# Two-engine first casts, unbroken fillers, W1 by row blocks and a new order of loads in an attention-plus-MLP kernel

## The chip, the cores and the metric

The kernel runs on one core of a Trainium2 chip. The core has a matrix engine (TensorE, PE in the profile; its weight loads are shown as PEld), three elementwise engines (VectorE: DVE, ScalarE: ACT, GpSimd: POOL), and queues that issue transfers, of which SyncE's (SP) carries nearly all here. The engines run side by side, each takes its own instructions in the order in which they were written, and semaphores hold one back until what it reads is there.

The metric is the device time of one execution in microseconds (us): the median of several runs. Times inside an execution come from one profiled execution and are counted from its first instruction.

## The reference

Eight batches, eight heads, 576 positions, head size 64. Sliding-window causal attention (each position sees itself and the 63 before it) is followed by a layer norm, a two-layer MLP with ReLU, and a residual:

```python
mask = (rel >= 0) & (rel < window)            # window = 64
scores = np.where(mask, scale * q @ k.T, -1e9)
x = softmax(scores) @ v                       # heads side by side: (8, 576, 512)
xn = (x - mean) / sqrt(var + 1e-6) * g_ln
out = x + relu(xn @ w_ch1) @ w_ch2            # 512 -> 2048 -> 512
```

Everything goes in and out in fp32; inside, the matmuls take fp16.

## The kernel before, in words

**Tiling.** Of each batch the first 512 positions are one group (g = 0 to 7) of four row blocks of 128 (kb or j = 0 to 3); the last 64 positions of all batches ("tails") make up a ninth group. For a group: `load_qk` and `load_v` fetch q, k, v in fp32, `cast_qk` and `cast_v` turn them into fp16 on POOL, `t_main` transposes q and k on PE and an elementwise engine copies the result out of PSUM (`evac`: 0 is ACT, 1 is DVE). `s_pe` makes the scores of one row block, `s_exp` the exponentials on ACT, `s_mask` the masking on DVE (in batch 0 a matmul with a bias masks instead: `pe_mask`). `b_pe` multiplies by the values; a ones column in the value tiles gives the softmax sum. `b_rows` on DVE does the division, the mean and the variance; `z_step` subtracts the mean, `zt_step` transposes the result on PE into zT. `s_mm` is `s_pe` with `s_exp`, `b_step` is `b_pe` with `b_rows`.

**Two value tiles.** A block's windows need the values in two alignments: vA holds the positions as they are, vB holds them shifted by 64. For batches 0 and 1 vB is filled by copies of half a tile (`vB_cur`, `vB_prev`) out of the fp32 staging v32; later batches do it with transfers.

**The MLP.** `mlp_units(g)` gives a list of units that PE does one after the other. For group 0: eight units `l1_half` (two hidden blocks of 128 for half of the positions, eight matmuls of 128x256), eight units `l1` (one hidden block for all 512 positions, four matmuls of 128x512), ten units `l2_three` (the second layer of row blocks 0 to 2, staggered, two to six matmuls of 128x512) and four of `l2` for row block 3. A ReLU on ACT empties each PSUM bank; there are two banks for it (`mm`).

**Order.** The schedule is written out by hand. Ahead of the main loop (lines 797 to 896) stand the loads, the casts and the whole attention of batch 0, but for the last value step. In the loop over groups, `at(i, f, ...)` puts a piece of the next batch's attention behind unit i. So with group 0's units go the transposes, scores and value steps of batch 1, with group 1's those of batch 2, and so on. `keep_clock(n)` puts n matmuls of 128x512 that nobody reads between pieces of batch 0's attention, where PE would sit still.

**W1 and W2.** W1 is loaded in eight pieces of 512 KB (`w1_load`), multiplied by the layer norm's gain gT and cast on POOL (`w1_cast`); gT is made on PE from the gain row (`gps`). Pieces 2q and 2q+1 are the upper and lower half of the rows of one quarter of the columns, so a hidden block of that quarter needs both. W2 follows in eight pieces (`w2_load`, `w2_cast`); the first four share four staging buffers with W1's first four, and the last one reuses the buffer of W2's first.

**SP's queue.** All these loads stand in one queue in program order, stores of the output too. In the kernel before, batch 1's first q, k and first half of v go ahead of W2, its second half behind it, batch 2's q and k after that, and batch 2's v behind group 0's first stores.

The functions that the change touches, and the main program, with the line numbers of the profile:

Of the kernel before, what the change touches and what calls it, by code (L numbers as in the profile page):

```python
# [20 lines left out]
def kernel(  # L21
# [10 lines left out]
    nc = tc.nc  # L32
# [88 lines left out]

    def cast_qk(b, half, xs=(0, 1)):
# [13 lines left out]

    def load_v(b, c0, c1):
        if c0 == 0:
            v32[b] = p_in.tile([128, 4, H, D], FP32, tag="v32", name=f"v32_{b}", bufs=1)
        for c in range(c0, c1):  # L140
            nc.sync.dma_start(
                out=v32[b][:, c],
                in_=v[b, :, 128 * c:128 * c + 128, :].rearrange("h s d -> s h d"),
            )

    def cast_v(b, c0, c1):
        nc.gpsimd.tensor_copy(out=vA[b][:, c0:c1, :, 0:D], in_=v32[b][:, c0:c1])
# [10 lines left out]
    def vB_cur(b, c, eng):  # L158
        evac(eng, vB[b][64:128, c, :, 0:D], v32[b][0:64, c])

    def vB_prev(b, c, eng):
        evac(eng, vB[b][0:64, c + 1, :, 0:D], v32[b][64:128, c])
# [12 lines left out]
    def w1_load(i):  # L175
        q2, pr = divmod(i, 2)
        if i < 4:
# [11 lines left out]
    def w1_cast(i):  # L189
        q2, pr = divmod(i, 2)  # L190
        t = wst.pop(("w1", i))
        dst = w1g[:, 2 * pr:2 * pr + 2, (HID // 4) * q2:(HID // 4) * (q2 + 1)]
# [158 lines left out]
    def b_rows(g, kb):  # L351
# [22 lines left out]
        if g < 2 and (g, kb) != (0, 2):  # L374
            z_step(g, kb)
# [74 lines left out]
    def mlp_units(g, split=0, three=False, seven=True):  # L450
# [157 lines left out]

        def l2_three(i):
# [129 lines left out]
        for half in range(2):  # L739
            for i in range(split // 2):  # L740
                units.append(lambda half=half, i=i: l1_half(half, i))
# [62 lines left out]
    for i in range(8):  # L804
        w1_load(i)
    make_identity(nc, ident16)
    nc.vector.memset(mask, 1.0)
# [14 lines left out]
    def keep_clock(n):  # L822
        m = mbias[:, :]
        mb = bass.AP(tensor=m.tensor, offset=m.offset, ap=[m.ap[0], [0, 8], m.ap[1]])
        for _ in range(n):
            nc.tensor.matmul(out=warm[:, :].rearrange("p (a i) -> p a i", i=64), lhsT=ident16, rhs=mb,  # L826
                             start=True, stop=True)

    keep_clock(4)
    gps = ps_mm.tile([128, DM], FP32, tag="mm", name="gps")  # L830
# [3 lines left out]
    nc.vector.tensor_copy(out=gT, in_=gps[:, 0:NKC])  # L834
    for b in range(2):
        alloc_qkT(b)
        alloc_v(b)
        init_vB(b)
    cast_qk(0, 0)
    cast_v(0, 0, 1)  # L840
    cast_v(0, 1, 2)
    cast_qk(0, 1)
    cast_v(0, 2, 3)
    cast_v(0, 3, 4)
    nc.gpsimd.tensor_copy(out=vB[0][64:128, 3, :, 0:D], in_=v32[0][0:64, 3])
    for i in range(8):
        w1_cast(i)

    keep_clock(1)
    t_main(0, 0, 0)  # L850
    keep_clock(2)
    t_main(0, 1, 0)
    keep_clock(4)
    s_mm(0, 0, True)
    vB_cur(0, 0, 1)
    vB_prev(0, 0, 1)
    vB_cur(0, 1, 1)
    vB_prev(0, 1, 1)
    keep_clock(3)
    s_mm(0, 1, True)  # L860
    b_step(0, 0)
    keep_clock(2)
    vB_cur(0, 2, 0)
    t_main(0, 0, 1, 0)
    keep_clock(1)
    t_main(0, 1, 1, 0)
    keep_clock(2)
    b_step(0, 1)
    keep_clock(2)
    vB_prev(0, 2, 0)  # L870
    s_mm(0, 2, True)
    zt_step(0, 0)
    b_step(0, 2)
    zt_step(0, 1)
    s_mm(0, 3, True)
    z_step(0, 2)


    load_qk(1, 0)
    load_v(1, 0, 2)  # L880
# [3 lines left out]
    cast_v(1, 0, 1)  # L884
    cast_v(1, 1, 2)
    for i in range(8):
        w2_cast(i)
        if i == 0:
            w2_load(7)
    load_qk(1, 1)  # L890
# [5 lines left out]
    load_qk(2, 1)  # L896

# [7 lines left out]
    for g in range(NGRP):  # L905
# [19 lines left out]
        if g == 0:  # L925
            at(0, b_step, 0, 3)
            at(1, zt_step, 0, 2)
            at(3, zt_step, 0, 3, "dve")
# [3 lines left out]
            at(13, vB_cur, 1, 0, 1)  # L932
            at(13, vB_prev, 1, 0, 1)
            at(13, vB_cur, 1, 1, 1)
            at(13, vB_prev, 1, 1, 1)
# [6 lines left out]
            at(19, b_pe, 1, 0)  # L942
            at(19, b_pe, 1, 1, "sc")
            at(19, b_rows, 1, 0)
            at(20, b_rows, 1, 1)
            at(21, zt_step, 1, 0)
            at(23, zt_step, 1, 1)
# [206 lines left out]
```

## Time and profile before

| | |
|---|---|
| median of 3 runs | 303.9 us (303.8 to 305.1) |
| the profiled execution's own time | 305.16 us |
| its span, first to last instruction | 303.4 us |
| PE busy | 292.2 us, 96% of the span |
| DVE, POOL, ACT busy | 217.9, 166.5, 153.2 us |
| PE idle ahead of its first matmul | 2.32 us |
| first W1 unit starts | 20.93 us |
| first `l1` unit starts | 29.78 us |
| first `l2_three` unit starts | 37.58 us |
| first unit of group 1 starts | 56.03 us |
| matmuls of `keep_clock` | 21 |

Busy is the time in which an engine has an instruction under way. In the lists by time, each row gives the start, the length (of a run of like instructions together, if several are merged), the engine, the line, what is written and read, and in brackets the idle time just before it and what ended that. A matmul's end is modelled, so in a run of matmuls the distance from one start to the next is the better measure. A cast that waited for "DMA" began when its transfer landed.

### The profile page before, as it was taken

The page shows a single profiled execution, that of the slowest core. Times are in us where ns is not written, and L with a number is a line of the kernel's source. Part 1 is how long each engine was busy: PE and PEld are TensorE (multiplying, and loading weights), DVE is VectorE, ACT ScalarE, POOL GpSimd, SP SyncE. Part 2 cuts the span into 40 slices and gives each one's busy share as a digit, 9 for nine tenths or more (in the row PEclk, how much of TensorE's full clock was granted, in tenths as well). Part 3 has the DMA queues.
Part 4 walks back from the last instruction along what each step waited for, and adds up shares of the span by engine and source line. Part 5 has one row for each costly group of instructions (what it writes and reads, how often), then busy time and mean ns, then how long its engine had stood idle before and what let it go on. Part 6 is the DMA issues. An engine that isn't in the chain of part 4 may idle for free.

```text
span 303.4 us, 7577 instructions
## 1 busy us (share of the span) xinstructions
PE 292.2 (96%) x3061; PEld 196.4 (65%) x3061; DVE 217.9 (72%) x418; ACT 153.2 (50%) x257; POOL 166.5 (55%) x251
## 2 busy tenths in 40 slices
PE   6999989899999999999999999999999999999992
PEld 4457445598455478646964686469646854788881
DVE  0588596765855897669766875698568775789972
ACT  1496635578447742875167528842574056306400
POOL 7579676462550898198809962888048407115200
PEclk9999999999999999999999999999999999999999
DMA  8999999989967998799189997992729396003014
GB/s 190 263 382 309 325 366 273 304 238 250 154 167 232 245 204 176 260 266 176 36 259 294 199 177 240 291 160 56 219 52 174 71 204 161 19 23 135 0 38 104
DMA packets 113893, 58.35 MB, mean 192 GB/s; under 512 B 83649, under 2 KB 104705, under 8 KB 113858
## 3 DMA queue, kind: packets, MB, share of 16 engines
q1 hardware_dynamic: 113056, 55.60, 75.6%
q0 software_dynamic: 512, 1.86, 2.5%
q8 instruction: 24, 0.39, 0.6%
q10 hardware_dynamic: 290, 0.40, 0.5%
q14 instruction: 11, 0.09, 0.1%
HBM read 38.80 MB, written 9.44 MB: 159 GB/s over the span
## 4 chain that ended last, share of the span: by engine, by line
PE 90%; DVE 5%; ACT 2%; issue 0%; POOL 0%; POOLq 0%
PE hps L459 30%; PE pA L536 12%; PE pB L536 8%; PE pC L536 8%; PE hph L601 7%; PE ch L471 5%; PE xps L348 4%; PE sc L304 3%; PE tp L234 3%; PE lA L656 2%; PE ch L618 2%; DVE vB L222 2%; PE warm L826 2%; DVE pt L321 1%; ACT pt L314 1%; PE lC L656 1%
## 5 line engine op out<-in xcount | busy, mean ns | idle before, releaser
L459 PE MATMUL hps<-zT,w1g 128*128 128x512 f16 x416 | 94.7, 379 | 0.0
L463 ACT ACTIVATE hrT<-hps 128x512 f16<-128x512 f32 x104 | 62.4, 600 | 41.2 <-PE hps L459 37.8
L459 PEld LDWEIGHTS <-w1g 128*128 128x128 f16 x416 | 39.2, 98 | 45.4 <-issue 2.2
L314 ACT ACTIVATE pt<-sc 128x512 f16<-128x512 f32 x72 | 39.3, 600 | 23.2 <-PE sc L304 22.5
L392 POOL TENSOR_SCALAR rsz<-mvg 128x1 f32<-128x1 f32 x28 | 10.8, 384 | 66.3 <-DVE mvg L373 58.8
L536 PEld LDWEIGHTS <-sS 128*128 128x128 f16 x448 | 43.3, 98 | 5.0
L128 POOL CAST qk<-qk 128x1024 f16<-128x1024 f32 x32 | 35.8, 1130 | 9.5 <-DMA qk<-in_q_dram 5.1
L321 DVE TENSOR_TENSOR pt<-pt,mask 128x1024 f16<-128x1024 f16 x32 | 26.0, 817 | 17.9 <-ACT pt L314 17.9
L536 PEld LDWEIGHTS <-hrT 128*128 128x128 f16 x336 | 32.1, 98 | 6.4 <-ACT hrT L463 1.0
L220 ACT COPY qkT<-tp 128x1024 f16<-128x1024 f16 x16 | 16.1, 1013 | 27.2 <-PE tp L234 23.7
L536 PE MATMUL pC<-w2s,sS 128*128 128x256 f16 x224 | 26.9, 273 | 0.0
L536 PE MATMUL pA<-wT,sS 128*128 128x256 f16 x224 | 26.9, 273 | 0.0
L368 DVE TENSOR_TENSOR xn<-xps,rcp 128x512 f32<-128x512 f32 (+1 forms) x48 | 25.7, 556 | 0.8
L370 DVE BATCH_NORM_STATS2 stats<-xn 128x6 f32<-128x512 f32 x36 | 25.0, 695 | 1.2
L510 DVE TENSOR_TENSOR sS<-hrT 128x512 f16<-128x512 f16 (+1 forms) x40 | 24.4, 609 | 2.1 <-ACT hrT L463 2.1
L601 PE MATMUL hph<-zT,w1g 128*128 128x256 f16 x192 | 23.2, 273 | 0.7 <-DVE zT L422 0.5
L393 POOL TENSOR_TENSOR rsz<-rsz,mhalf 128x1 f32<-128x1 f32 x28 | 19.7, 704 | 2.3
L601 PEld LDWEIGHTS <-w1g 128*128 128x128 f16 x192 | 18.1, 98 | 3.4 <-DVE zT L422 0.7
L398 POOL TENSOR_SCALAR z<-xn,rsz 128x512 f16<-128x512 f32 x24 | 18.5, 771 | 2.5
L471 PE MATMUL ch<-w2s,hrT 128*128 128x512 f16 x80 | 18.8, 380 | 0.0
L348 PEld LDWEIGHTS <-pt 128*64 128x64 f16 x576 | 11.4, 110 | 11.0 <-issue 5.3
L364 DVE RECIPROCAL rcp<-xps 128x8 f32<-128x8 f32 (+1 forms) x48 | 7.8, 183 | 15.0 <-PE xps L348 14.9
(117 smaller groups left out, 445.4 us busy)
## 6 DMA issues: line engine op xcount, KB each, us to landing
out_dram<-xn SPq DMA_DIRECT2D x33, 256.0 KB, 2.5
qk<-in_q_dram SPq DMA_DIRECT2D x16, 512.0 KB, 5.5
qk<-in_k_dram SPq DMA_DIRECT2D x16, 512.0 KB, 6.8
v<-in_v_dram SPq DMA_DIRECT2D x32, 256.0 KB, 6.3
w2s<-in_moe_w_ch_dram SPq DMA_DIRECT2D x9, 512.0 KB, 9.4
w1s<-in_moe_w_ch_dram SPq DMA_DIRECT2D x4, 512.0 KB, 6.7
tk<-in_k_dram SPq DMA_DIRECT2D x8, 256.0 KB, 4.9
tv<-in_v_dram SPq DMA_DIRECT2D x8, 256.0 KB, 4.8
```

The costliest lines, as they stand in the source:

```text
L128: nc.gpsimd.tensor_copy(out=dst[:, :].rearrange("p (a j) e d -> p a e j d", j=j), in_=t[:, :].rearrange("p (a e j d) -> p a e j d", e=2, j ...
L314: nc.scalar.activation(out=o, in_=i, func=AF.Exp, bias=0.0, scale=scale)
L321: nc.vector.tensor_tensor(out=ptv, in0=ptv, in1=mb, op=ALU.mult)
L348: nc.tensor.matmul(out=tiles[h // n][64 * r:64 * r + 64, h % n, :D + 1], lhsT=pt[:, par, hp, r, :], rhs=rhs, start=True, stop=True)
L368: nc.vector.tensor_tensor(out=xn[:, n * i:n * i + n], in0=xps[:, :, 0:D], in1=rcp_b, op=ALU.mult)
L370: nc.vector.bn_stats(out=stats, in_=xv)
L459: nc.tensor.matmul(out=hps, lhsT=w1g[:, kc, 128 * hc:128 * (hc + 1)], rhs=zT[g][:, kc, :], start=(kc == 0), stop=(kc == NKC - 1),)
L463: nc.scalar.activation(out=hrT[:, hc, :], in_=hps, func=AF.Relu, bias=0.0, scale=1.0)
L471: nc.tensor.matmul(out=ch[kb], lhsT=hrT[:, hc, 128 * kb:128 * (kb + 1)], rhs=w2s[:, hc, :], start=(hc == 0), stop=(hc == NHC - 1),)
L510: nc.vector.tensor_tensor(out=o, in0=x, in1=y, op=op)
L536: nc.tensor.matmul(out=o, lhsT=a[:, c, 128 * p:128 * p + 128], rhs=wv[:, c, :], start=(first and (p == 0 or split_c) and c == 0), stop=(c ...
L601: nc.tensor.matmul(out=hps[:, e], lhsT=w1g[:, kc, 128 * hc:128 * (hc + 1)], rhs=zT[g][:, kc, 256 * half:256 * half + 256], start=(kc == 0) ...
```

## The change

There are six edits.

1. **First casts.** `cast_two` casts batch 0's first q and k in two halves, one on ACT and one on DVE, in place of POOL; `t_two` transposes each half into a tile of its own, and ACT and DVE copy one half each.
2. **Fillers.** `keep_clock` uses a tile of zeros (`wfill`) that DVE sets right at the start, both as weights and as data, in place of the identity and the mask's bias. Thirteen of them stand ahead of the first transpose; the others are moved. There are 28 in all.
3. **Batch 0's attention is reordered.** The first value step is ahead of the second score step, the gain's matmuls are behind it, the gain is copied by ACT, zT of blocks 0 to 3 is copied by DVE, the last value step is ahead of the units. POOL fills more of vB (four half-tile copies instead of one).
4. **W1 by row blocks.** Pieces 2 and 3 of W1 hold all 512 rows of an eighth of the columns each (256 columns), so that each serves two hidden blocks alone; POOL casts such a piece in four instructions of 128x256. Two of group 0's units become `l1_rows`: four hidden blocks for one row block of 128 positions (16 matmuls of 128x128).
5. **W2 ahead of batch 1's v, value steps in pairs.** In SP's and POOL's order W2's eight pieces come ahead of batch 1's v. The copies into vB for batch 1 go from DVE to ACT, behind unit 20; both first value steps go behind unit 22 (before: 19), and the scores of its last two blocks behind unit 29 (before: 28). Batch 1's last two value steps stand together behind unit 1 of group 1 (before: behind units 0 and 2). The subtractions of the mean for blocks 0 and 1 are placed on their own, the second one behind two residual additions on DVE.
6. **Batch 2's v.** It is loaded into the staging tiles of the tails (`tk32`, `tv32`), which are free then, right behind batch 2's q and k and ahead of group 0's stores; before it was behind the first three stores.

The diff, cut to its core:

```diff
+    def cast_two(b, x, half):
+        t = qk32.pop((b, x, half))
+        dst = p_in.tile([128, 8, 2, D], FP16, tag=f"qk16_{x}", name=f"qk16_{x}_{b}_{half}")
...
+        for a in range(2):
+            evac(a, o[:, 2 * a:2 * a + 2], i[:, 2 * a:2 * a + 2])
+    def t_two(b, x, half):
...
+        for a in range(2):
+            tp = t_tile([128, 4, 128], f"tp_{b}_{x}_{half}_{a}")
+            for i in range(4):
+                nc.tensor.transpose(out=tp[:, i, :], in_=src[:, 4 * a + i], identity=ident16)
+            evac(a, qkT[b][x][:, 2 * a:2 * a + 2, c0:c0 + 256].rearrange("c h (p j) -> c h p j", j=2),
+                 tp[:, :].rearrange("c (h j) p -> c h p j", j=2))
...
     def load_v(b, c0, c1):
-        if c0 == 0:
-            v32[b] = p_in.tile([128, 4, H, D], FP32, tag="v32", name=f"v32_{b}", bufs=1)
+        if c0 == 0 and b == 2:
+            v32[b] = [p_in.tile([128, 2, H, D], FP32, tag=tag, name=f"v32_{b}_{tag}", bufs=1) for tag in ("tk32", "tv32")]
+        elif c0 == 0:
+            v32[b] = [p_in.tile([128, 4, H, D], FP32, tag="v32", name=f"v32_{b}", bufs=1)]
...
     def w1_load(i):
+        if i in (2, 3):
+            t = p_wst.tile([128, NKC, HID // 8], FP32, tag="wld", name=f"w1s_{i}")[:, :, :]
+            wst[("w1", i)] = t
+            nc.sync.dma_start(
+                out=t, in_=moe_w_ch1[:, (HID // 8) * i:(HID // 8) * (i + 1)].rearrange("(c p) n -> p c n", p=128),
+            )
+            return
     def w1_cast(i):
+        if i in (2, 3):
+            for kc in range(NKC):
+                nc.gpsimd.tensor_scalar(out=w1g[:, kc, (HID // 8) * i:(HID // 8) * (i + 1)], in0=t[:, kc],
+                                        scalar1=gT[:, kc:kc + 1], scalar2=1.0, op0=ALU.mult, op1=ALU.mult)
+            return
...
-        if g < 2 and (g, kb) != (0, 2):
+        if g < 2 and (g, kb) not in ((0, 2), (1, 0), (1, 1)):
             z_step(g, kb)
+        def l1_rows(kb):
+            for i in range(2):
+                if kb == 2:
+                    rows_ps[i] = ps_mm.tile([128, 2, 256], FP32, tag="mm", name=f"hph_{g}_1_{i}")
+                c0 = 128 * (kb - 2)
+                for e in range(2):
+                    hc = 2 * i + e
+                    for kc in range(NKC):
+                        nc.tensor.matmul(
+                            out=rows_ps[i][:, e, c0:c0 + 128], lhsT=w1g[:, kc, 128 * hc:128 * (hc + 1)],
+                            rhs=zT[g][:, kc, 128 * kb:128 * kb + 128], start=(kc == 0), stop=(kc == NKC - 1),
+                        )
+                if kb == 3:
+                    nc.scalar.activation(out=hrT[:, 2 * i:2 * i + 2, 256:512], in_=rows_ps[i],
+                                         func=AF.Relu, bias=0.0, scale=1.0)
...
+        halves = [(half, i) for half in range(2) for i in range(split // 2)]
+        if g == 0:
+            halves = [(0, 0), (0, 1), (0, 2), 2, 3, (0, 3), (1, 2), (1, 3)]
...
     load_qk(1, 0)
-    load_v(1, 0, 2)
     for i in range(7):
         w2_load(i)
     cast_qk(1, 0)
-    cast_v(1, 0, 1)
-    cast_v(1, 1, 2)
     for i in range(8):
         w2_cast(i)
         if i == 0:
             w2_load(7)
+    load_v(1, 0, 2)
+    cast_v(1, 0, 1)
+    cast_v(1, 1, 2)
...
     load_qk(2, 1)
+    load_v(2, 0, 4)
...
         if g == 0:
-            at(0, b_step, 0, 3)
-            at(1, zt_step, 0, 2)
-            at(3, zt_step, 0, 3, "dve")
+            at(1, zt_step, 0, 2, "dve")
+            at(2, zt_step, 0, 3, "dve")
...
-            at(13, vB_cur, 1, 0, 1)
-            at(13, vB_prev, 1, 0, 1)
-            at(13, vB_cur, 1, 1, 1)
-            at(13, vB_prev, 1, 1, 1)
...
-            at(19, b_pe, 1, 0)
-            at(19, b_pe, 1, 1, "sc")
-            at(19, b_rows, 1, 0)
-            at(20, b_rows, 1, 1)
-            at(21, zt_step, 1, 0)
-            at(23, zt_step, 1, 1)
+            for c in range(2):
+                at(20, vB_cur, 1, c, 0)
+                at(20, vB_prev, 1, c, 0)
+            at(22, b_pe, 1, 0)
+            at(22, b_pe, 1, 1, "sc")
+            at(22, b_rows, 1, 0)
+            at(22, z_step, 1, 0)
+            at(23, b_rows, 1, 1)
+            at(24, zt_step, 1, 0)
+            at(25, z_step, 1, 1)
+            at(26, zt_step, 1, 1)
...
-            at(28, s_pe, 1, 2)
-            at(28, s_pe, 1, 3, False, "t")
+            at(29, s_pe, 1, 2)
+            at(29, s_pe, 1, 3, False, "t")
...
-            at(27, load_v, 2, 0, 4)
         if g == 1:
-            at(0, b_step, 1, 2)
-            at(2, b_step, 1, 3)
+            at(1, b_pe, 1, 2)
+            at(1, b_pe, 1, 3, "sc")
+            at(1, b_rows, 1, 2)
+            at(2, b_rows, 1, 3)
```

Batch 0's stretch after the change, in the order in which it is written (its calls alone): `keep_clock(13)`, `cast_two` and `t_two` of q, `keep_clock(4)`, `cast_two` and `t_two` of k, `keep_clock(1)`, POOL's casts, `s_mm(0, 0)`, three copies into vB, `keep_clock(3)`, `b_step(0, 0)`, `s_mm(0, 1)`, the gain, W1's casts, `t_main` of q's second half, `keep_clock(1)`, `b_step(0, 1)`, `t_main` of k's second half, `zt_step(0, 0)`, `keep_clock(2)`, `s_mm(0, 2)`, `zt_step(0, 1)`, `keep_clock(1)`, `b_step(0, 2)`, `s_mm(0, 3)`, `z_step(0, 2)`, `keep_clock(3)`, `b_step(0, 3)`.

## The prediction

> **What bounds the kernel now.** I read the busy rows first, then PE's instructions in order of time up to 60 us with the idle time before each, then the chain of waits, then POOL's casts (they tell when transfers land) and DVE's order.
>
> ```profile
> PE 292.2 (96%) x3061; PEld 196.4 (65%) x3061; DVE 217.9 (72%) x418; ACT 153.2 (50%) x257; POOL 166.5 (55%) x251
> DMA  8999999989967998799189997992729396003014
> ```
>
> PE is the bound, and transfers are busy without a break for the first eleven slices (83 us). PE's own order:
>
> ```profile
> 2.32 1.86 PE L826 MATMUL warm<-mbias,ident 128*128 128x512 f16 x4 [2.32 <-DVE mbias L819]
> ...
> 14.30 0.61 PE L826 MATMUL warm<-mbias,ident 128*128 128x512 f16 x2
> ...
> 20.93 1.05 PE L601 MATMUL hph<-zT,w1g 128*128 128x256 f16 x8
> ...
> 26.27 3.67 PE L601 MATMUL hph<-zT,w1g 128*128 128x256 f16 x32 [0.52 <-DVE zT L422]
> ...
> 43.54 0.22 PE L348 MATMUL xps<-vB,pt 128*64 128x65 f16 x1 [0.86 <-DVE pt L321]
> ...
> 57.66 0.22 PE L348 MATMUL xps<-vB,pt 128*64 128x65 f16 x1 [0.59 <-DVE pt L321]
> ...
> 58.32 1.91 PE L601 MATMUL hph<-zT,w1g 128*128 128x256 f16 x16 [0.21 <-DVE xn L481]
> ```
>
> Up to 20.9 us PE mostly fills time; from 26.3 it lacks 0.86, 0.59 and 0.21 us, and after 58.3 the list shows no idle time above 0.06 us. So only the time at which PE gets past about 60 us can change, and the end moves by as much. The landings, in POOL's list:
>
> ```profile
> 9.29 0.62 POOL L147 CAST vA<-v 128x512 f16<-128x512 f32 x1 [0.55 <-DMA v<-in_v_dram]
> ...
> 20.85 2.72 POOL L195 TENSOR_SCALAR w1g<-w1s,gT 128x512 f16<-128x512 f32 x4 [1.36 <-DMA w1s<-in_moe_w_ch_dram]
> ...
> 45.43 1.04 POOL L209 CAST w2s<-w2s 128x1024 f16<-128x1024 f32 x1 [1.04 <-DMA w2s<-in_moe_w_ch_dram]
> 47.18 1.04 POOL L128 CAST qk<-qk 128x1024 f16<-128x1024 f32 x1 [0.71 <-DMA qk<-in_q_dram]
> ```
>
> POOL waits for nearly every piece up to 57 us: the queue of transfers, not POOL, sets when W2 and batch 1 are there.
>
> **Part 1, first casts and fillers (edits 1, 2).** Fillers before run at 0.45 us each (four from 2.32 to 4.12), at 14.30 at 0.22. Now they need only DVE's memset and start at 1.1 us, not 2.32. Thirteen end at 1.1 + 13 x 0.45 = 6.95 if all are slow, at 3.96 if all are fast. q lands at 5.0 (POOL's first cast starts at 5.08); half a cast is 128x512, 0.62 (64x512 on ACT or DVE) to 0.72 (ACT's z of 128x512), so q's transposes start between 5.8 and 6.95; before 6.31. k lands at 6.9; cast, two transposes of four (0.22 to 0.43 each) and half copies (0.57 ACT, 0.42 DVE) give the first scores at 8.7 to 9.7 instead of 11.57: 1.9 to 2.9 us.
>
> [...]
>
> **Part 2, batch 0 to the units (edit 3).** A block costs DVE 2.44 us (14.41 to 16.85: reciprocal to z). The first value step comes after its own exponentials (two in 1.08), at 10.3 to 11.3 against 13.92. Then: gain matmuls (1.79 at the slow pace), q's second half (lands at 11.1, POOL casts to 12.2), value step 1 at 13.7 to 14.9, z of block 1 after 16.6 to 17.8, k's second half copied by ACT at 15.6, scores 2 at 15.7, value step 2 at 17.2 to 18.1, scores 3 and their exponentials, value step 3 at 19.65 to 20.55. So the first unit can start at 20.05 to 20.95. POOL's other chain: v's last piece lands at 15.2; three more half copies (0.61 each) end at 17.2 where the one before ended at 16.56; W1's first two pieces (2.71) are cast at 19.95. This hides behind PE's chain. The first unit is hardly earlier (20.93), but the value step (0.4 and a 0.26 wait) and the 0.52 stall are out of the units.
>
> **Part 3, W1 (edit 4).** Unit 0,2 needs piece 2 alone: landed 20.8, four casts of 128x256 (half of 0.69 each; at worst the whole, +1.4 us on POOL, which meets `l1` with no slack), ready at 22.3 when PE wants it at 22.0. Two units of 16 matmuls of 128x128 at 0.056 (eight transposes in 0.45) are 1.79 against 1.75 for those they replace. Eight units of 0.87, two zT transposes (0.45) and 0.3 of waits: `l1` starts at 27.8 to 28.7 against 29.78. **Gain so far 1.1 to 2.0; I take 1.7.**
>
> Piece rows shrink from 2 to 1 KB. From 50 to 58 us, with batch 2's 1 KB rows, the transfers moved 348 GB/s, from 35 to 43, W2's 2 KB rows, 389: a piece takes 1.51 instead of 1.35 us, so two pieces put 0.3 us on everything behind. [...]
>
> **Part 4, W2 and batch 1 (edit 5).** From 27.8: eight `l1` (0.863 each) and two transposes end at 35.6; units 16 to 22 are 36 matmuls of 0.216, 7.8, scores 0.57: **PE reaches batch 1's value steps at 43.95** (up to 44.9). W2 lands about two v pieces earlier (1.17 each, 8.12 to 9.29), so each of its casts ends 0.5 us or more before its unit. But v now is what comes last. All up to W2's piece 7 landed at 45.4 before, v included, so v's first piece lands at 45.4 - 1.17 + 0.3 = 44.5 at the latest end. At the early end 43.4: the transfers moved only 225 GB/s from 27 to 32 us, when SP spent 24.35 to 29.43 on issuing v's small pieces; if that gap (0.8 to 1.1 us) closes, all come sooner. The late end is made of the same loads' rows, so I take 44.1. ACT's half cast (0.62) and 0.1 of signalling: **value step 0 at 44.8, 0.85 us after PE is there.** The second one waits for the second piece and ACT's third copy: 46.0.
>
> Behind it the chain lies on DVE: from 45.25, block 0 (1.95, as 43.41 to 45.38), a residual addition (0.70), block 1 (1.88), two additions (1.40), the small subtraction (0.10): 51.3; z on ACT (0.72 and 0.1): zT of block 1 can be transposed at 52.1. PE's own work would bring it there at 46.4 + 1.30 + 0.86 + 0.22 + 0.43 + 0.45 + 0.86 = 50.5: **a wait of 1.6 us that was not there before** (z was ready at 48.3, PE came at 49.34). Queued behind it on PE are units 27 to 29, on ACT the copy of q's second half. Then 0.22 + 0.86 + 0.45 + 1.73 = 55.35, scores; four exponentials end at 57.8, the last mask (0.82 to 1.46) at 58.7 to 59.3, the last value step (0.45) at 59.15 to 59.75. Before, the same work (both value steps, two units of group 1) was done at 60.54 - 0.87 = 59.67. **Sum: -0.5 to +0.1, I take -0.3.** DVE's vB copies (4.11 us at 36.45, the wait of 0.86) are gone, but what they delayed now waits for v.
>
> **Part 5, batch 2's v (edit 6).** Nothing: its cast stands behind rstdg at 63.24 on POOL, later than any landing. The stores move back by up to 6.7 us (four v issues, 53.55 to 60.22); batch 2's rows that need their buffers start at 74.85.
>
> The sum is made against the profiled execution: 305.16, span 303.4, the 1.8 around it unchanged, so 304.9. That execution was 1.26 above the median of the runs; against 303.9 the change gives **303.6**. A measurement here tells about 0.5% (1.5 us) from no change.
>
> **Rivals.**
> *The early gain is kept.* If v lands before 43.3, the first wait goes: value step 0 at 43.95, all 0.85 earlier, 302.7. If the DVE chain does not bind either, another 1.6: 301.1, and near 300.3 if the 1.66 of old waits is lost whole. For: the gap at 27 to 32 us. Against: 6.9 us of DVE and ACT work stand against 4.1 of PE between the same two points. Chance of 302.4 or less 0.2.
> *v lands late (slower).* v's issue is now behind that of W2's last piece, which waits for W2's first cast; then come 256 B rows, and batch 1's q is served beside them. If v comes with q, at 47.1 (POOL's row at 47.18), value step 0 starts at 47.8, 3 us later: 306.6. It decides from 45.9 on (1.5 us more than forecast plus the 0.3). For: W2's last piece took 9.9 us from issue (35.52) to cast. Against: the queue works in order wherever POOL's rows show it. Chance 0.17.
> *The clock stays slow.* Zeros might not count as work. Then PE's steps from 9 to 20 us double (about 3 us on its chain) and the units run slow until real work has opened the clock, some 7 us (as from 5.9 to 13 before; half lost: 3.5); less the 0.85 of slack: +5.6, 309.2. The trace has no matmul on zeros. Chance 0.07.
> *Forecast*, 0.56: 302.5 to 304.9 (v from 43.4 to 44.5, late start of the units, the mask's two prices).
>
> **Numbers.** Faster by 0.5%: the first rival, 0.20. Slower: the next two, 0.24. Same: 0.56. The range leaves out the ends of both sides: 302.0 to 306.3.
>
> **What would show it.** Fillers at 1.1 us and the pace of 0.22 before 8 us; first unit near 20.5; `l1` near 28; POOL's W2 casts about 2 us earlier and v's behind them at 44; an idle row ahead of the first value step of batch 1 (vB by ACT), one of 1 to 2 us ahead of block 1's zT transposes (z by ACT); group 1's third unit near 59.5. It is wrong if that unit starts off by more than 1.5 us, or if idle time appears after 60 us.

## The result and the profile after

| | before | after |
|---|---|---|
| median | 303.93 us (10 runs, 303.46 to 305.1) | 305.55 us (10 runs, 305.33 to 306.51) |
| ratio | | 1.0057, 95% interval 1.0044 to 1.007 |
| the profiled execution's own time, span | 305.16, 303.4 | 306.51, 304.7 |

The change makes the kernel slower by 1.62 us. The forecast was 303.6, no change; the time lies in its range, but on the other side of the median before.

The busy rows of the profile after, which answer to the first fence of the prediction:

```profile
PE 292.0 (96%) x3084; PEld 195.6 (64%) x3084; DVE 212.9 (70%) x420; ACT 154.9 (51%) x261; POOL 168.6 (55%) x256
DMA  8999999999877999999489996992719496003014
```

TensorE is busy as long as before, with 23 matmuls more; transfers fill the first ten slices. TensorE's own order after the change, in the list by time (start, length, what; in brackets the idle time before and what ended it):

```profile
1.11 4.88 PE L888 MATMUL warm<-wfill 128*128 128x512 f16 x13 [1.11 <-DVE wfill L868]
5.83 0.61 PE L137 MATMUL tp<-ident,qk 128*128 128x128 f16 x8
...
8.71 0.50 PE L341 MATMUL sc<-qkT,qkT 64*128 64x64 f16 x16
...
20.38 1.92 PE L638 MATMUL hph<-zT,w1g 128*128 128x256 f16 x16
...
28.44 1.89 PE L496 MATMUL hps<-zT,w1g 128*128 128x512 f16 x8
...
45.76 0.19 PE L385 MATMUL xps<-vB,pt 128*64 128x65 f16 x1 [0.46 <-ACT vB L257]
...
52.12 0.40 PE L454 MATMUL ztp<-ident,z 128*128 128x128 f16 x4 [1.28 <-ACT z L425]
...
58.50 0.22 PE L385 MATMUL xps<-vB,pt 128*64 128x65 f16 x1 [0.52 <-DVE pt L358]
...
59.48 2.79 PE L638 MATMUL hph<-zT,w1g 128*128 128x256 f16 x24
...
155.57 2.78 PE L496 MATMUL hps<-zT,w1g 128*128 128x512 f16 x12 [1.27 <-issue]
```

Up to group 1's third unit (59.48) it runs much as the prediction had it. Then comes what the prediction had excluded: an idle row after 60 us, 1.27 us ahead of group 4's first unit. The landings, from GpSimd's list after the change:

```profile
17.64 2.70 POOL L232 TENSOR_SCALAR w1g<-w1s,gT 128x512 f16<-128x512 f32 x4
20.34 3.82 POOL L226 TENSOR_SCALAR w1g<-w1s,gT 128x256 f16<-128x256 f32 x8
...
43.23 1.04 POOL L246 CAST w2s<-w2s 128x1024 f16<-128x1024 f32 x1 [0.40 <-DMA w2s<-in_moe_w_ch_dram]
44.21 1.17 POOL L172 CAST vA<-v 128x512 f16<-128x512 f32 x2
```

W2's last cast starts at 43.23 instead of 45.43, and v lands behind it (first piece 43.78, second 44.68).

For comparing profiles I use one mark at which both kernels have done the same work: the start of group 1's fifth unit, behind all of batch 1's value steps. It stands at 61.43 us in the shown profile of before and at 61.24 after. So in these two executions the change is 0.19 us ahead at the mark, loses 1.45 us up to the unit at 155.57 (it started at 154.31 before), and ends 1.3 behind in span.

That is an account of two executions, and it isn't yet one of the medians: the shown execution of before was 1.23 us above the median, the one after 0.96.

### The profile page after: what moved, and what is told of

Read it like the earlier page. It is cut to its first block, busy times and chain, and to the rows that moved or that the text cites. A ratio compares the mean times of both kernels' runs of the same rounds, so it can differ in the third digit from the quotient of the medians.

```text
span 304.7 us, 7638 instructions
## 1 busy us (share of the span) xinstructions
PE 292.0 (96%) x3084; PEld 195.6 (64%) x3084; DVE 212.9 (70%) x420; ACT 154.9 (51%) x261; POOL 168.6 (55%) x256
## 4 chain that ended last, share of the span: by engine, by line
PE 89%; DVE 3%; DMA 2%; SPq 2%; ACT 2%; issue 1%; POOL 0%; ACTq 0%
PE hps L496 30%; PE pA L573 12%; PE pB L573 8%; PE pC L573 8%; PE hph L638 6%; PE ch L508 5%; PE xps L385 4%; PE sc L341 3%; PE tp L271 3%; PE ch L673 3%; PE lA L711 2%; DMA qk<-in_k_dram 2%; PE lC L711 1%; ACT pt L351 1%; SPq L166 1%; SPq L89 1%
## 5 line engine op out<-in xcount | busy, mean ns | idle before, releaser
L496 PEld LDWEIGHTS <-w1g 128*128 128x128 f16 x416 | 39.1, 98 | 47.0 <-issue 3.7
L429 POOL TENSOR_SCALAR rsz<-mvg 128x1 f32<-128x1 f32 x28 | 10.1, 360 | 66.5 <-DVE mvg L410 59.2
L147 POOL CAST qk<-qk 128x1024 f16<-128x1024 f32 x30 | 34.8, 1172 | 9.1 <-DMA qk<-in_q_dram 5.2
L358 DVE TENSOR_TENSOR pt<-pt,mask 128x1024 f16<-128x1024 f16 x32 | 24.1, 759 | 20.0 <-ACT pt L351 20.0
L257 ACT COPY qkT<-tp 128x1024 f16<-128x1024 f16 (+1 forms) x17 | 16.3, 961 | 23.9 <-PE tp L271 19.3
L405 DVE TENSOR_TENSOR xn<-xps,rcp 128x256 f32<-128x256 f32 (+1 forms) x49 | 25.7, 547 | 0.8
L401 DVE RECIPROCAL rcp<-xps 128x4 f32<-128x4 f32 (+1 forms) x49 | 7.9, 183 | 20.6 <-PE xps L385 20.5
L638 PE MATMUL hph<-zT,w1g 128*128 128x256 f16 x176 | 21.1, 273 | 0.2 <-ACT hrT L659 0.2
L435 POOL TENSOR_SCALAR z<-xn,rsz 128x512 f16<-128x512 f32 x24 | 19.9, 830 | 2.5
L638 PEld LDWEIGHTS <-w1g 128*128 128x128 f16 x176 | 16.6, 98 | 2.4 <-POOL w1g L232 0.4
```

What stands on the lines that cost most here:

```text
L147: nc.gpsimd.tensor_copy(out=dst[:, :].rearrange("p (a j) e d -> p a e j d", j=j), in_=t[:, :].rearrange("p (a e j d) -> p a e j d", e=2, j ...
L358: nc.vector.tensor_tensor(out=ptv, in0=ptv, in1=mb, op=ALU.mult)
L405: nc.vector.tensor_tensor(out=xn[:, n * i:n * i + n], in0=xps[:, :, 0:D], in1=rcp_b, op=ALU.mult)
L496: nc.tensor.matmul(out=hps, lhsT=w1g[:, kc, 128 * hc:128 * (hc + 1)], rhs=zT[g][:, kc, :], start=(kc == 0), stop=(kc == NKC - 1),)
L638: nc.tensor.matmul(out=hps[:, e], lhsT=w1g[:, kc, 128 * hc:128 * (hc + 1)], rhs=zT[g][:, kc, 256 * half:256 * half + 256], start=(kc == 0) ...
```

## The experiments

Five readings were on trial; a "draw" is one execution out of many. **Theory 1:** the loss is the idle row at 155.57. That unit needs block 3 of group 4's z, which a transposing transfer puts into zT. It was issued at 149.78 before and 150.05 after, and landed at 153.32 and 155.48; one that ran alone took 2.39 (issued at 144.32 before). In the trace's list of packets, an instruction fetch (16 KB; the queue "instruction" has 24 of them before, for 6122 matmuls and weight loads, one per 255, so I take them for TensorE's) ran at 154.02 before and at 151.15 to 152.50 after; the changed program has 46 more instructions ahead of it. Packets of the transpose that started at 151.8 ended only at 153.4. **Rival 2:** the transfer is late because of the new order of loads and of z. **Theory 3:** the shown execution of before was a late draw, by the clock's opening. **Rival 4:** the clock always opens at 11.9. **Theory 5:** the fifth edit (v behind W2, value steps late and as a pair) costs what the others gain, and the waits of the shown profile of before came from DVE's instructions meeting GpSimd's.

The first four kernels keep the transposing transfers.

### Shifting the fetch

```diff
-    keep_clock(13)                    # the changed kernel
+    keep_clock(13, 8)                 # 8 of the 13 as four matmuls of 128 columns each
```

> The changed kernel with 8 of its first 13 filler matmuls (512 columns each) cut into four of 128 columns, on other columns of the same throw-away tile: the same columns streamed, 24 more matmuls and 24 more weight loads in TensorE's program (48 instructions), nothing else moved. Theory 1 (the 1.27 us that TensorE loses at 155.57 us come from a 16 KB instruction fetch of TensorE, seen at 151.15 to 152.50 us, which holds up the transfer that transposes block 3 of group 4, issued 150.05, landed 155.48): fetches come every 256 instructions, here some 24 instructions per us, so all come about 2 us earlier in the work, this one near 149.2; the transfer then takes 2.4 to 3.6 us, lands by 153.7, TensorE does not wait at group 4's first unit, and the time is 304.3 (305.55 - 1.27). Rival 2 (the transfer is late because GpSimd wrote z 0.27 us later and the queues of transfers stand differently since v and W2 changed places): nothing of that is touched, the transfer takes over 5 us again and the time stays at 305.5.

Measured: 305.31 us (7 runs, 305.07 to 305.35). The fetch came at 148.81, the transfer landed at 153.43 (3.55 us), and the wait was gone; TensorE's list by time:

```profile
152.66 1.92 PE L573 MATMUL pC<-w2s,sS 128*128 128x256 f16 x16
154.42 2.78 PE L496 MATMUL hps<-zT,w1g 128*128 128x512 f16 x12
```

Theory 1 holds for the mechanism and falls for the size. In the median 0.24 us is gained, not 1.27.

The same edit on the kernel before, where it moves a fetch into the transfer:

```diff
-    keep_clock(4)                     # the kernel before, at both places
+    keep_clock(4, 4)
-    keep_clock(3)
+    keep_clock(3, 2)
```

> The kernel before with 10 of its fillers (the four first, the four ahead of the first scores, two of the next three) cut into four matmuls of 128 columns each: 30 more matmuls and weight loads, 60 instructions, nothing else moved. Theory 1: TensorE's fetch at 154.02 us comes 60 instructions earlier, some 2.8 us, near 151.2, into the transposing transfer that was issued at 149.78 and landed at 153.32 undisturbed; it lands near 155.2, TensorE, which wants it at 154.48, waits about 0.7 to 1.0 us, and the time is 304.6 to 304.9 against 303.9. Rival 2: 303.9, no wait at group 4's first unit.

Measured: 306.33 us (8 runs, 304.21 to 306.46) against 303.86, ratio 1.0063 (1.0041 to 1.0085). In the profile (305.07 us) the fetch came at 149.86 into a transfer issued at 148.95, which took 5.18 us, and TensorE waited:

```profile
151.74 1.92 PE L536 MATMUL pC<-w2s,sS 128*128 128x256 f16 x16
154.23 2.78 PE L459 MATMUL hps<-zT,w1g 128*128 128x512 f16 x12 [0.57 <-PE pC L536]
```

(In the shown profile of before the unit started at 154.31, not at 154.48 as I had it.) So a few filler matmuls at the start can cost the kernel before 2.5 us. The profile shows 0.57 of them; the slower executions were not profiled, and where the rest lies stays open. This profile held the first hint for theory 3: it passed the mark at 60.60, 0.83 us ahead of the shown one, though the same program but for cut fillers.

### Taking the transfer away, and the last edit

```diff
-        if XZ <= g and not (kb == 3 and g in (3, 5)):
+        if XZ <= g and not (kb == 3 and g in (3, 4, 5)):
```

> The changed kernel with block 3 of group 4's z transposed by TensorE (four 128x128 transposes and a copy by ScalarE) instead of by a transfer, as groups 3 and 5 have it. Both theories agree that the wait at group 4's first unit depends on that transfer: z is written at 150.02, TensorE adds 0.22 us of transposes, and the copy (0.6) is done before 154; the wait of 1.27 is gone: 305.55 - 1.27 + 0.22 = 304.5. A third reading, that the wait belongs to something else of that unit (a PSUM buffer, a weight), would leave 305.5 or more.

Measured: 307.14 us (5 runs, 307.05 to 307.26). The wait didn't go; it moved ahead of the transposes, in slot 23, where TensorE now waits for z itself:

```profile
150.07 0.40 PE L454 MATMUL ztp<-ident,z 128*128 128x128 f16 x4 [1.24 <-POOL z L435]
```

My expectation had asked when z is ready, and not when TensorE comes to the slot: it comes 1.24 us earlier. The transfer had hidden that distance.

```diff
-    load_v(2, 0, 4)                   # behind batch 2's q and k, into the tails' staging
+            at(27, load_v, 2, 0, 4)   # group 0's slot 27, into v's own buffer
```

> The changed kernel with the last edit undone: batch 2's v again in the buffer of v, and loaded in group 0's slot 27, as before the change. By the prediction this edit is worth nothing, and by theory 1 the fetch and the late transfer stay: 305.5, with the wait at group 4's first unit. By rival 2 the order of the transfers decides, and this puts a part of it back: the transfer lands near 153.3 and the time is near 304.3.

Measured: 305.68 us (6 runs, 305.26 to 306.49). The last edit is worth nothing, as forecast, and rival 2 gets no support. The profile (305.26) has the fetch at 151.86, the landing at 154.37 and no idle row at 154.46, where the unit starts. A late landing need not stall the kernel, and the span of the shown execution, 304.7, is the longest of the changed kernel's ten (the others 303.5 to 304.1): its 1.27 us are no measure of the median.

### Without the transposing transfers

Three of the changed kernel's profiles passed the mark at 61.24 to 61.53 and had spans of 303.5 where nothing stalled, while the kernel before had spans of 301.3 to 302.6 in 14 runs, against 303.4 in the shown one. (In 30 later runs it had 301.2 to 303.2, and once 306.2: a draw as late as the shown one is rare, but it is not alone.) So most of the loss had to lie ahead of the mark, against other executions of before than the shown one. To take late transposes out of the question, the next kernels are twins in which TensorE does every transpose. They are slower by some 20 us, all behind 61 us, and their first 60 us are the program in question:

```diff
-    XQ = 3
-    XZ = 2
+    XQ = 9
+    XZ = 9
-            if i >= 2:                # t_tail, both places
+            if i >= 9:
-                at((2, 14, 18, {3: 25, 5: 25}.get(b, 23))[j], zt_step, b, j)
+                at((6, 14, 18, 25)[j], zt_step, b, j)
```

> The kernel before with every transposing transfer replaced by TensorE's transposes and a copy by ScalarE (q from batch 3 on, z from batch 2 on, the last tails), and the first block of a group's z transposed in slot 6 instead of 2. It computes the same. All of that lies after 76 us, so the first 60 us are those of the kernel before, and no transfer that an instruction fetch could hold up feeds TensorE's units. It is slower in itself: about 190 transposes at 0.055 us, 10 us, and some waits for copies: 312 to 325, no bearing on the theories. What bears on them: theory 3 (the shown profile of the kernel before drew a late opening of the clock, 11.89 us; its other executions open earlier, and that is why their spans are 301.3 to 302.6 against 303.4): this profile shows another opening, 8.4 to 11.9 us, and the spans of its executions spread by 1 us or more. Rival 4 (the clock always opens at 11.9 and the executions differ by late transfers): 11.9 again, and a spread below 0.5 us, for there is no such transfer.

> The changed kernel with the same replacement. Theory 1 alone (the change is 0.2 to 0.3 us ahead at 60 us and loses 1.27 by a transfer that comes late after a fetch): no such transfer here, so 0.2 to 0.3 us faster than the kernel before with the replacement, or at most equal. Theory 3 (against the median execution of the kernel before, the change is already 1.0 to 1.6 us behind at 60 us, the fetch adds its part only in some executions): 1.0 to 1.6 us slower than the median of the kernel before with the replacement, spans spread by 0.5 us or less, clock open by 7.1 us.

> The kernel before with the replacement, unchanged, profiled a second time, and timed in as many rounds again. It parts two readings of the forecast's miss. Reading A: the shown execution of before was a late draw in its first 60 us (third unit of group 1 at 59.19; 57.87 in the first profile with the replacement, whose first 60 us are the same program), because DVE's copies and masks met GpSimd's casts; then this draw too has its third unit well ahead of 59.19, at 57.2 to 58.6, waits between 40 and 60 us of 0.2 to 0.8 us together instead of 1.66, and among the executions the span follows that unit. Reading B: 59.19 is the usual time, and the first profile with the replacement was an early draw: 58.8 to 59.5 here, waits of 1.4 to 1.9 us.

"Clock opens" is the first entry at full rate in the trace's record of the granted clock; times in us.

| | median (range), runs | clock opens | first `l1` | waits 26.4 to 60.6 us | mark |
|---|---|---|---|---|---|
| before, as shown | 303.93 | 11.89 | 29.78 | 1.75 | 61.43 |
| twin of before | 324.80 (323.93 to 326.52), 5 | 8.89 | 29.61 | 0.66 | 60.38 |
| twin of before, second time | 323.98 (323.65 to 324.53), 6 | 9.41 | 29.40 | 0.38 | 59.81 |
| after, as shown | 305.55 | 4.99 | 28.44 | 2.65 | 61.24 |
| twin of after | 325.66 (324.92 to 326.02), 5 | 5.19 | 28.66 | 2.87 | 61.51 |

The twin of after is 1.18 us slower than the eleven runs of the other twin (median 324.48), with no transposing transfer in either: theory 1 alone had it faster. The shown execution of before is the odd one, and reading A of the last expectation holds: the third unit of group 1 starts at 59.19 us in it, and at 57.87 and 57.57 in the two profiles of the twin. These two executions took 324.56 and 324.48 us, at the median of the eleven, so they stand for the usual one. (That the span follows that unit does not hold so finely: both spans are 322.8, with marks 0.57 apart.) Three other draws of its first 60 us, the one with cut fillers among them, pass the mark at 59.81 to 60.60, those of the changed kernel, five of them, at 61.24 to 61.69. But theory 3 had the wrong reason. The clock opened 2.5 to 3 us earlier in the twins, which is worth 0.2 to 0.4 us at the first `l1`. The rest is waits behind it. DVE's list by time, first in the shown execution of before:

```profile
36.45 4.11 DVE L222 CAST vB<-v 64x512 f16<-64x512 f32 x4
40.58 2.91 DVE L321 TENSOR_TENSOR pt<-pt,mask 128x1024 f16<-128x1024 f16 x2
...
56.15 1.46 DVE L321 TENSOR_TENSOR pt<-pt,mask 128x1024 f16<-128x1024 f16 x1 [1.62 <-ACT pt L314]
```

and in the second profile of its twin, the same instructions:

```profile
36.07 2.47 DVE L222 CAST vB<-v 64x512 f16<-64x512 f32 x4
39.35 0.76 DVE L321 TENSOR_TENSOR pt<-pt,mask 128x1024 f16<-128x1024 f16 x1 [0.81 <-ACT pt L314]
40.33 1.22 DVE L321 TENSOR_TENSOR pt<-pt,mask 128x1024 f16<-128x1024 f16 x1 [0.22 <-ACT pt L314]
...
55.30 0.69 DVE L321 TENSOR_TENSOR pt<-pt,mask 128x1024 f16<-128x1024 f16 x1 [1.96 <-ACT pt L314]
```

One instruction has two prices. Over the fifteen profiles, each of the 17 half copies of v during which GpSimd did nothing took 0.42 to 0.43 us, and the dearest of those that met GpSimd's work 1.31; a mask took 0.68 or 0.69 undisturbed (191 times) and up to 1.52. GpSimd's casts of W2 start as the pieces land (seven of the eight waited 0.19 to 1.04 us for a transfer in the shown profile of before), so small shifts of the landings change who meets whom. The shown execution drew the dear ones and had 1.75 us of waits, 1.45 of them ended by a mask. The copies seem to decide for the first wait: in the first profile of the twin the two masks behind them were nearly as dear (1.38 and 1.52), but the copies took 3.21 us instead of 4.11, the masks were done 1.1 us earlier, and TensorE did not wait for them. The second twin has a single wait above 0.15 us in that stretch:

```profile
39.62 2.90 PE L618 MATMUL ch<-w2s,hrT 128*128 128x512 f16 x12 [0.28 <-POOL w2s L209]
```

What holds such an instruction up was not shown, only that GpSimd was at work: in the shown execution of before the mask at 41.97 met it for 1.24 us and took 1.52, 0.83 more than 0.69; but a copy at 37.77 met it from start to end and took 0.43.

### The edits apart

The fillers alone, on the twin of before:

```diff
-    keep_clock(4)
+    keep_clock(13)                    # on a tile of zeros that DVE writes first
```

> The kernel before with the replacement and the fillers of the change alone: DVE writes a tile of zeros first, the fillers read it, the first block has 13 instead of 4; casts, value steps, W1, W2 and v stand as before the change. Theory 3: the clock opens by 7 us in every execution, so the times spread by 0.5 us or less, but the median is within 0.6 us of that of the kernel before with the replacement, whose median execution opens early too; TensorE waits about 1 us for W2's pieces near 42 us, which eats what is left. If an opening near 11.9 were the rule: 0.8 to 1.5 us faster than it.

Measured: 324.47 us (4 runs, 323.59 to 324.66). The clock opened at 6.82, the first `l1` started at 29.51, the mark was passed at 59.39. The median is as expected, the spread (1.07) is not narrow: an early opening of the clock alone doesn't make executions agree.

The changed kernel's twin without the fifth edit:

```diff
     load_qk(1, 0)
+    load_v(1, 0, 2)
     ...                               # W2's loads and casts
-    load_v(1, 0, 2)
-            at(22, b_pe, 1, 0)        # and all of group 0's slots from 13 on, as before
+            at(19, b_pe, 1, 0)
```

> The changed kernel with the replacement and without the fifth edit: batch 1's v loaded and cast ahead of W2 again, its copies on DVE in slot 13, its value steps in slots 19 and 20 and the rest of group 0's slots as before the change; casts, fillers, W1's row blocks and batch 2's v as changed. Theory 3 with the fifth edit as the place of the loss (v's wait, 0.46 us, and the wait for block 1's z, 1.3 us): the value steps come near 42.5, W2's last pieces make TensorE wait about 1 us instead, and it is 0.5 to 1.5 us faster than the changed kernel with the replacement. If W2's pieces cost as much as v's do (W2's last cast ended at 46.5 in the shown profile of before, its unit would want it near 42.5), both are the same within 0.4 us, and transfers are the bound to 45 us in whichever order they come.

Measured: 324.25 us (4 runs, 323.92 to 324.50), 1.41 us less than with it (325.66), and no run of the one meets a run of the other. Mark 59.66. TensorE's waits in the list by time, first the twin with the fifth edit (all of them from 44 to 62 us), then the one without:

```profile
48.37 0.40 PE L454 MATMUL ztp<-ident,z 128*128 128x128 f16 x4 [0.40 <-ACT z L425]
49.44 0.61 PE L271 MATMUL tp<-ident,qk 128*128 128x128 f16 x8 [0.24 <-ACT zT L457]
52.26 0.40 PE L454 MATMUL ztp<-ident,z 128*128 128x128 f16 x4 [1.35 <-ACT z L425]
59.37 0.22 PE L385 MATMUL xps<-vB,pt 128*64 128x65 f16 x1 [0.87 <-DVE pt L358]
```

```profile
39.48 2.90 PE L673 MATMUL ch<-w2s,hrT 128*128 128x512 f16 x12 [0.62 <-POOL w2s L246]
```

With the fifth edit 2.86 us of waits follow from the late value steps, without it 0.62 and two small ones for W2 and a residual. Which half of the edit does it? The loads as before, the slots as changed:

```diff
     load_qk(1, 0)
+    load_v(1, 0, 2)                   # ahead of W2; value steps stay in slots 22 and 23
```

> The changed kernel with the replacement, the loads and casts of batch 1's v ahead of W2 as before the change, but the fifth edit's slots kept (value steps as a pair in slots 22 and 23, copies on ScalarE in slot 20). It parts the fifth edit in two. If the late slots are the loss (two blocks' row work on DVE, 3.8 us, and three residual additions, 2.1, between the value steps and z, with only 4 us of units beside them), the wait for block 1's z stays at 1.0 to 1.4 us, waits for W2's pieces of 0.7 us come on top, and the time is 325.7 to 326.4. If v's late landing is the loss, the wait of 0.2 to 0.5 us ahead of the second value step goes and the z follows it: 324.6 to 325.2.

Measured: 328.22 us (5 runs, 326.78 to 328.55); in the profile, the fastest of the five, the mark is at 62.55 and the late chain's waits are all there, with W2's added:

```profile
37.79 1.02 PE L673 MATMUL ch<-w2s,hrT 128*128 128x512 f16 x4 [0.23 <-POOL w2s L246]
39.34 7.22 PE L673 MATMUL ch<-w2s,hrT 128*128 128x512 f16 x30 [0.52 <-POOL w2s L246]
...
53.75 0.40 PE L454 MATMUL ztp<-ident,z 128*128 128x128 f16 x4 [1.36 <-ACT z L425]
```

With v there early (its pieces landed at 32.31 and 33.14, 13 us before the value steps) z's wait is as long as without (1.36 against 1.35), and in the twin of after, too, no wait above 0.15 us is ended by a copy of v. So the wait comes from the late slots, not from v's landing. What stands between the value steps and that z is in DVE's list of the shown execution of after, without a pause:

```profile
45.34 0.21 DVE L401 RECIPROCAL rcp<-xps 128x8 f32<-128x8 f32 x1 [4.82 <-PE xps L385]
...
47.33 0.74 DVE L518 SCALAR_TENSOR_TENSOR xn<-ch,rstdg,xn 128x512 f32<-128x512 f32 x1
...
49.81 1.38 DVE L518 SCALAR_TENSOR_TENSOR xn<-ch,rstdg,xn 128x512 f32<-128x512 f32 x2
51.11 0.14 DVE L424 TENSOR_SCALAR nmu<-mvg 128x1 f32<-128x1 f32 x1
```

L518 is a residual addition: three of them and the row work of two blocks. The median of this kernel, 328.22, lies 1.4 us above the profiled execution and above both expectations; that was not profiled and stays open.

One call moved in the twin of after, so that z no longer stands behind both residual additions:

```diff
             at(24, zt_step, 1, 0)
+            at(24, z_step, 1, 1)
-            at(25, z_step, 1, 1)
```

> The changed kernel with the replacement and one call moved: block 1's z of batch 1 in slot 24, behind the copy of block 0's zT and ahead of one of the two residual additions, instead of slot 25 behind both. Theory 5 (the fifth edit makes DVE's chain from the value steps to that z the bound near 52 us, where TensorE waits 1.35 us): nmu comes one addition (0.70) earlier, z is ready near 51.5 instead of 52.2, the wait shrinks to about 0.65, and the time is 0.5 to 0.7 us below the changed kernel with the replacement (325.66): 325.0. Rival: the mask's wait near 58 us (0.87) grows by what is gained, for the masks meet GpSimd's casts: 325.5 to 325.7.

Measured: 325.04 us (4 runs, 324.60 to 325.53), mark 60.62. The wait shrank as expected, and the masks' wait did not grow:

```profile
51.83 0.40 PE L454 MATMUL ztp<-ident,z 128*128 128x128 f16 x4 [0.69 <-ACT z L425]
...
57.88 0.22 PE L385 MATMUL xps<-vB,pt 128*64 128x65 f16 x1 [0.18 <-DVE pt L358]
```

The loads by need, on the twin without the fifth edit:

```diff
+    for i in range(3):
+        w2_load(i)
     load_v(1, 0, 2)
-    for i in range(7):
+    for i in range(3, 7):
         w2_load(i)
```

> The changed kernel with the replacement, without the fifth edit's slots, and with batch 1's first two pieces of v between W2's third and fourth piece (loads and casts alike) instead of ahead of all of W2 or behind it. If transfers bound the stretch to 45 us in either order, their order can be set by need: TensorE wants W2's pieces 0 to 2 from 36.5 us on (without the fifth edit it waits 0.14 and 0.62 us for pieces 1 and 2), v only for the copies ahead of the value steps at 42. v's pieces land near 36.5 and 38, the copies (2.4 to 4.1 us on DVE) and masks end by 41.5 to 43: the 0.76 us of waits go, and the time is 323.5 (324.25 - 0.76). Rival: v now is late for its copies, the masks behind them on DVE end after 42, a wait of 0.5 to 1.0 us comes back ahead of the value steps: 324.2 to 324.6.

Measured: 324.00 us (5 runs, 323.40 to 324.95). Of W2's waits 0.21 us is left (and 0.15 ahead of a value step), the mark is at 59.04, the earliest of all. In the median it isn't told apart from 324.25. These two twins are the best found, 0.2 and 0.5 us below the eleven runs of the twin of before; with transposing transfers they were not tried, nor was the kernel before itself profiled again.

Last, the four half copies on ScalarE, on the twin of before:

```diff
-            at(13, vB_cur, 1, 0, 1)   # and the other three
+            at(13, vB_cur, 1, 0, 0)
```

> The kernel before with the replacement, and batch 1's four half copies of v in slot 13 on ScalarE (0.62 us each there) instead of DVE. Theory 5 (the waits of the shown profile of before at 43.54, 57.66 and 58.32 us, 1.66 us together, came from copies and masks on DVE that took 1.1 to 1.5 us each where GpSimd was casting at the time, and 0.42 and 0.69 where it was not, which differs by execution): the masks at 39 to 42 start 2 to 3 us earlier and are done before TensorE wants them whatever they cost, no wait ahead of batch 1's first two value steps is left, and the median is 0.2 to 0.6 us below the kernel before with the replacement (324.80), the spread below 1.5 us. Rival: those copies do not matter in the median execution, and the spread (323.9 to 326.5) comes from elsewhere: 324.6 to 325.0; or ScalarE's copies hold up its rectified units and exponentials, which are queued behind them: 325 or more.

Measured: 327.80 us (5 runs, 326.85 to 328.12), against theory 5's expectation and as the rival's second half had it. ScalarE's list and TensorE's:

```profile
36.56 2.51 ACT L220 CAST vB<-v 64x512 f16<-64x512 f32 x4
38.98 1.07 ACT L463 ACTIVATE hrT<-hps 128x512 f16<-128x512 f32 x2
```

```profile
39.62 0.60 PE L618 MATMUL ch<-w2s,hrT 128*128 128x512 f16 x2 [1.99 <-ACT hrT L463]
```

The rectified units stood behind the copies. The price was more than the 1.99 us (the mark is at 63.34, 2.96 behind the later of the twin's two), and the busy times by stretch tell why (in order: the stretch, its length, PE, PEld, DVE, ACT and POOL with the number of instructions, then the granted clock, the transfers' share and GB/s):

```profile
34.00:40.80 6.80, 4.81 (x58) 2.43 (x57) 2.22 (x2) 4.78 (x9) 4.17 (x4) 1.00 0.99 354
40.80:44.30 3.50, 3.50 (x9) 1.25 (x10) 2.20 (x2) 1.93 (x4) 2.70 (x3) 0.51 1.07 384
44.30:50.00 5.70, 5.70 (x58) 2.71 (x57) 3.36 (x10) 0.72 (x1) 3.71 (x4) 1.00 1.20 255
```

From 40.83 to 44.24 us the clock was granted at half. The other runs fit: those two of the five with a mean granted clock of 0.994 and 0.996 took 327.08 and 326.85 us, the three with 0.990 and 0.991 took 327.80 to 328.12. It stays untested by this whether the copies' price on DVE matters in the median execution; that rests on the profiles compared above.

## Why the prediction was wrong

**The step that failed** is the last one of the working: "That execution was 1.26 above the median of the runs; against 303.9 the change gives 303.6." It takes the excess of the shown execution for something that the change leaves alone. The excess lay in the stretch that the change rewrites: 1.05 us at the mark (61.43 against 60.38, the middle of the three other draws), mostly in waits ended by the DVE mask (0.86 and 0.59). The first of them has no counterpart in the changed schedule, in place of the second it waits 0.52 and 0.15. So the change was credited with waits that the kernel before doesn't have in its usual execution. The sum against the profiled execution, 304.9, is 0.65 from the measured 305.55.

**"So only the time at which PE gets past about 60 us can change, and the end moves by as much"** failed too. A transfer at 150 us had 0.99 us to spare in the shown profile of before (landed 153.32, the unit started at 154.31), and a fetch at 151.15 instead of 154.02, with 46 more instructions ahead of it, used that up in the shown execution of after (landed 155.48). In the changed kernel this costs 0.24 us in the median (with the fetch moved: 305.31) and 1.27 in the shown execution.

**The sum as measured.** At the mark the changed kernel is 1.13 us behind (61.51 against 60.38, the middle draws), and the fetch adds 0.24: 1.37 of 1.62. The rest, 0.25, is below what the draws can tell and stays open.

**Parts 1 to 3** held against the shown profile: fillers from 1.11 (1.1), 0.43 us apart up to 4.93 and 0.22 from 5.18 on (the clock opened at 4.99; "before 8 us" was my estimate, no row of before shows it), q's transposes at 5.83 (5.8 to 6.95), first scores at 8.71 (8.7 to 9.7), first unit at 20.38 (20.05 to 20.95), `l1` at 28.44 (27.8 to 28.7, 1.34 us gained where I took 1.7). Only the four value steps came a little before their bounds (9.90, 13.35, 17.07 and 19.54). W1's casts of 128x256 took 0.48 each, between half and the whole of 0.69. Pieces with rows of 1 KB landed 1.50 us apart (18.76, 20.26, 21.76), those with 2 KB rows 1.36 (23.12, 24.48), as the estimate from the rows had it (1.51 and 1.35). But the gain is not what it seemed. Edits 1 to 4 and 6 together (the twin without the fifth) give 0.23 us against the twin of before.

**Part 4** held step by step: v landed at 43.78 (43.4 to 44.5), the second value step started at 45.76 (46.0), block 1's transposes at 52.12 (52.1) after a wait of 1.28 (1.6), group 1's third unit at 59.48 ("near 59.5"). Only the wait of 0.85 ahead of the first value step didn't come: TensorE was there at 44.78, late enough. Its judgement failed: "Sum: -0.5 to +0.1" set these waits against the waits of one execution. Undone by itself, this part gives 1.41 us back.

**Part 5** held: nothing.

**The rivals.** The early gain is kept: no, the chain on DVE was the bound, as the argument against it said. v late: slower came true, by another mechanism; v was on time. The clock stays slow with zeros: no, in all ten profiles with unbroken zero fillers it opened between 4.99 and 7.14 us; what sets the time within these 2.15 us was not shown.

## What to carry to other kernels

Before subtracting a profiled execution's excess over the median, find the rows that make it: here the execution stood above the other two runs (305.1 against 303.8 and 303.9), and it priced one DVE instruction at 0.69 and at 1.46 us. If those rows lie where the change works, the excess belongs to the change's gain and has to be taken off it. And a step moved later for the sake of a transfer drags its whole chain along: here 3.8 us of row work and three residual additions came to stand between two value steps and the next thing that TensorE needs from them.

## What the runs showed of the hardware

- The instruction fetches taken for TensorE's are packets of 16 KB that took 0.89 to 1.73 us in the shown profiles of before and after; the kernel before has 24 of them for 6122 matmuls and weight loads, one per 255. A transposing transfer of z took 2.39 us where nothing else moved (issued at 144.32 before); that of block 3 of group 4 took 3.54 and 3.55 beside GpSimd's transfers (two profiles), and 4.54 to 5.43 with a fetch inside as well (three). 48 or 60 instructions put in 140 us earlier decided which.
- In one execution, that with the half copies on ScalarE, the clock was granted at half for 3.41 us (40.83 to 44.24), from 1.2 us after the end of a TensorE wait of 1.99 us on. Behind none of the waits in the other fourteen profiles, up to 1.36 us once the clock was open, was it granted at half before the last 4 us of the span.
- With gaps between the fillers the clock opened at 8.81 to 11.89 us (five profiles, first filler at 2.3 to 2.9 us); without gaps, from 1.1 us on, at 4.99 to 7.14.
